# One transfer for a pair's values, and transposed keys written four columns apart

## The chip, the cores and the metric

The kernel runs on one core of a Trainium2 chip. The metric is the device time of one execution in microseconds. Three executions of the kernel before took 689.19, 692.28 and 689.82 us; their median is 689.82.

## What is computed

A block of attention, in which neighbouring queries are averaged two by two, is followed by a mixture-of-depths layer. Cut to what matters:

```
q, k, v: (8, 8, 1152, 64) float32          # batch, heads, sequence, head size
q_pool = q.reshape(B, H, S // 2, 2, D).mean(axis=3)
scores = (1 / sqrt(D)) * q_pool @ k.T      # 576 x 1152 per head
attn   = softmax(scores)
x      = (attn @ v), heads side by side    # (8, 576, 512)
score  = x @ w_gate                        # one number for a token
for each batch: the 128 tokens of highest score
    x[token] += sigmoid(score) * (relu(x[token] @ w1) @ w2)
```

A sum over all 1,152 keys does not depend on the order of the keys, as long as scores and values have the same one. The change rests on that.

## The kernel before, in words

**Pairs and half-steps.** Two heads of a batch form a pair: 8 batches of 4 pairs give 32 pairs. Each pair is worked in two halves of 288 pooled queries, so the main loop in `run` has 64 half-steps `h`. In each, TensorE multiplies keys by queries (`scores`, line 869, 36 products into nine PSUM tiles); ScalarE takes the exponential of each tile (line 876); and TensorE multiplies the half before by the values (`weighted`, line 887). Keys are taken in nine groups `c` of 128: of each group, columns `c * 128` to `c * 128 + 127` of the tile `kT` (partitions: head and feature) are the stationary operand of the scores, and the same 128 keys lie along the partitions of the tile `v_sb`, at index `c`. So column `c * 128 + m` of `kT` and row `m` of `v_sb[:, :, c, :]` must be the same key.

**Order.** The order is written out by hand: an engine does its instructions in the order in which `run` calls the functions. VectorE's share of a half-step is, in order: routing work placed at "mid" (`units`), a reduction for the gate (line 1035), two sums of exponentials by a transposing reduction (`folded`, line 913, each near 1.95 us) and a small sum (line 923), routing work placed at "sums", then in every first half `added` (line 944) and `prepare_pair` of the next pair, then the transpose of the outputs (`drained`, line 966). GpSimd adds exponentials (line 908), pools queries (line 767) and adds the two halves of the outputs (line 897).

**Preparing a pair.** `prepare_pair` is called in the first half-step of the pair before: GpSimd adds neighbouring queries into `qp`, VectorE transposes the keys `kb` into `kT` in blocks of 32 x 32 (line 770), then `qp` into `qT` (line 774). Their scores begin two half-steps later. There are 31 such pairs; the first one is prepared by other code (`load_first`, `prepare_first`), with TensorE's transposes, and its values come in by line 807 in natural order.

**Transfers.** Nearly all are issued by SP, in the order of the calls: in every second half-step the keys of the pair after the next (four transfers, line 742), its queries (four, line 745), the next pair's values (`load_values`, four, line 756), and the results of an earlier pair (four stores, line 1024). In between come the small transfers of routing: `row<-total` and its way back (lines 1094 to 1098), `row_rank<-both` and `lines<-row_rank` (1194 and 1198), `copy<-xe` and its way back (1269 and 1282). Some of these wait for VectorE, or for the transfer just before them, and SP waits with them. `kb` and `v_sb` have two buffers, `qb` has one.

**Routing.** When the four pairs of a batch are done, its tokens are ranked on VectorE (lines 1145 to 1192, result `both`), written to memory and read back as `lines`, searched (line 1229), and the chosen rows fetched. The fetched rows of most batches are transposed by VectorE into `xeT` (line 1284). Two batches at a time then pass through seven products per layer on TensorE (line 1437), with sums on GpSimd (line 1403) and VectorE (line 1450).

**Where a key goes.** In `kb` partition `i` of a block of 32 holds 36 keys in a row, key `i * 36 + n`, and the change's code reads `n` as `g * 9 + c` with `g` of 0 to 3. Block `(c, g)` is transposed as one 32 x 32 block. Before, its 32 columns are written side by side, at `c * 128 + g * 32 + i`, so row `g * 32 + i` of the values must hold key `i * 36 + g * 9 + c`. That is why the values come by four transfers, one for each `g`, each over 32 partitions.

Of the kernel before, what the change touches and what calls it, by code (L numbers as in the profile page):

```python
# [10 lines left out]
P = 128  # L11
BLK = 32
# [15 lines left out]
def _any_scores(  # L28
# [451 lines left out]
    in_pair = [(j, t) for j in range(2) for t in range(NF)] + [(0, NF)]  # L480
    upcoming = load_pair(*pairs[0])
    run(prepare_pair(upcoming))
    preparing = iter(())
    routing = iter(())
# [23 lines left out]
    for n, (b, hp) in enumerate(pairs):  # L508
        pair = upcoming
        run(preparing)  # L510
        if hp == 0:
            x = xpool.tile([P, NT, Dm], F32, name="x")
        for i, (j, t) in enumerate(in_pair):
            now = {"pair": pair, "j": j, "t": t, "x": x}
            advance(now)
            if two is not None and two["t"] == NF and two["pair"]["hp"] == NPAIR - 1:
                run(routing)
                routing = routed(two["pair"]["b"], two["x"])
            one, two = now, one
            if i == 0 and n + 1 < len(pairs):  # L520
                upcoming = load_pair(*pairs[n + 1])
                preparing = prepare_pair(upcoming)
            if n == 0 and i == 0:
                load_weights()
            if i >= 3:
                next(preparing, None)
            next(routing, None)
# [7 lines left out]
class _Plain:  # L535
# [212 lines left out]
    def load_values(self, pair):  # L748


        nc, hp = self.nc, pair["hp"]
        v_sb = pair["v"] = self.load.tile([P, 2, self.NC, self.D], F32, name="v_sb", bufs=2)
        of = self.v[pair["b"], 2 * hp : 2 * hp + 2]
        of = of.rearrange("j (i g c) d -> g i j c d", i=BLK, c=self.NC)
        for g in range(P // BLK):
            nc.sync.dma_start(
                v_sb[g * BLK : (g + 1) * BLK, :, :, :].rearrange("i j c d -> i j (c d)"),
                of[g].rearrange("i j c d -> i j (c d)"),
            )

    def prepare_pair(self, pair):

        nc = self.nc
        qp = self.load.tile([P, self.QB, BLK], F32, name="qp", bufs=1)
        kT = pair["kT"] = self.load.tile([P, self.S], F32, name="kT")
        qT = pair["qT"] = self.load.tile([P, self.Sp], F32, name="qT")
        nc.gpsimd.tensor_tensor(  # L767
            out=qp[:, :, :], in0=pair["q"][:, :, 0, :], in1=pair["q"][:, :, 1, :], op=ALU.add
        )
        nc.vector.transpose(  # L770
            kT.rearrange("p (c g i) -> p c g i", c=self.NC, i=BLK),
            pair["k"].rearrange("p (g c) d -> p c g d", c=self.NC),
        )
        nc.vector.transpose(qT[:, :], qp.rearrange("p n d -> p (n d)"))  # L774
# [971 lines left out]
```

## Time and profile before

The profiled execution took 689.66 us, of which the profile's span covers 687.9. The page gives the busy time of each engine, and then the costliest groups of instructions: for each a line of the program, the engine, what it writes and reads, how often, the busy time in all, the mean of one, and the idle time of the engine just before them with what ended it.

| what | number |
|---|---|
| span; profiled execution; median of three | 687.9; 689.66; 689.82 us |
| TensorE's granted clock over the span | 0.998 |
| ScalarE, exponentials (L876), 576 | 320.4 us, 699 ns each |
| TensorE, values (L887) and scores (L869), 4,608 each | 296.7 and 296.4 us, 403 ns each |
| VectorE, transposing reductions (L913), 128 | 250.7 us, near 1.96 us each |
| VectorE, transpose of queries (L774), 31 | 22.6 us, 730 ns each |
| values' transfers (L756), 124 of 144 KB | median 3.5 us from issue to landing |
| keys' transfers (L742), 124 of 144 KB | median 4.5 us |
| DMA moved over the span | 101.22 MB, 147 GB/s |

Instructions of TensorE overlap, so their busy times add up to more than its stretch of time, and its busy share is no measure of its efficiency. Idle time before an instruction matters only where the engine is the one that the rest waits for.

### The profile page before, as it was taken

To read this page: it belongs to the slowest core of one execution; us is meant where nothing else is said; L and a number is where in the kernel's file an instruction comes from. 1 tells how busy PE (TensorE), PEld (TensorE's weight loads), DVE (VectorE), ACT (ScalarE), POOL (GpSimd) and SP (SyncE) were. 2 spreads that over 40 slices of the span, in tenths; PEclk is the share of its full clock that TensorE was granted. 3 is DMA by queue.
4 is the path that set the end of the run, shared out by engine and by line. 5 is a ranking of instruction groups with operands and counts; after the bars stand their busy time and mean duration, and the time that the engine had idled before them with its cause. 6 is when DMAs were issued, how large, how long until landed. Compare 5 with 4: busy or idle time off the path is not lost.

```text
span 687.9 us, 23660 instructions
## 1 busy us (share of the span) xinstructions
PE 678.0 (99%) x9972; PEld 564.4 (82%) x9972; DVE 536.4 (78%) x842; ACT 457.7 (67%) x998; POOL 512.9 (75%) x503
## 2 busy tenths in 40 slices
PE   9999999999999999999999999999999999999996
PEld 6668899989997998786888899777788899867776
DVE  3867888998999796786698977695879989688930
ACT  5677777777777783847777677583877777575220
POOL 4788888798887775867996978483999888569241
PEclk9999999999999999999999999999999999999999
DMA  9888878688779767953878787783777777644311
GB/s 173 158 176 182 209 143 202 130 155 165 138 167 171 159 136 140 229 101 80 227 129 176 135 166 148 139 197 64 158 190 171 140 152 163 118 116 118 81 47 36
DMA packets 397059, 101.22 MB, mean 147 GB/s; under 512 B 377232, under 2 KB 381200, under 8 KB 395664
## 3 DMA queue, kind: packets, MB, share of 16 engines
q1 hardware_dynamic: 395408, 95.13, 67.1%
q0 software_dynamic: 1296, 4.20, 1.9%
q8 instruction: 80, 1.31, 0.8%
q10 hardware_dynamic: 240, 0.30, 0.2%
q14 instruction: 35, 0.29, 0.1%
HBM read 81.97 MB, written 17.62 MB: 145 GB/s over the span
## 4 chain that ended last, share of the span: by engine, by line
PE 83%; DVE 4%; DMA 4%; issue 4%; POOL 3%; ACT 1%; SPq 0%; POOLq 0%; DVEq 0%; ACTq 0%
PE ps L887 36%; PE ps L869 36%; PE ps L1437 8%; DVE fold L913 2%; DMA out_dram<-xe,index 1%; PE ps L1312 1%; POOL acc L908 1%; ACT p L876 1%; DMA v_sb<-in_v_dram 1%; DMA lines<-row_rank 1%; PE ps L616 1%; DMA row_rank<-both 0%; POOL prod L976 0%; POOL s L1403 0%; DVE pick L1164 0%
## 5 line engine op out<-in xcount | busy, mean ns | idle before, releaser
L876 ACT ACTIVATE p<-ps 128x576 f32<-128x576 f32 x576 | 320.4, 699 | 2.4 <-PE ps L869 2.4
L887 PE MATMUL ps<-p,v_sb 64*64 64x288 f32 x4608 | 296.7, 403 | 2.0 <-DMA v_sb<-in_v_dram 2.0
L869 PE MATMUL ps<-qT,kT 64*64 64x288 f32 x4608 | 296.4, 403 | 0.7 <-DVE token L637 0.5
L908 POOL TENSOR_TENSOR acc<-p 128x576 f32<-128x576 f32 x192 | 272.0, 1444 | 26.7 <-ACT p L876 26.1
L887 PEld LDWEIGHTS ps<-p,v_sb 64*64 64x64 f32 x4608 | 233.7, 133 | 49.9 <-ACT p L876 13.3
L869 PEld LDWEIGHTS ps<-qT,kT 64*64 64x64 f32 x4608 | 229.3, 133 | 51.4 <-ACT p L876 4.6
L913 DVE TRANSPOSE_TENSOR_REDUCE fold<-p 128x54 f32<-128x1728 f32 x64 | 126.0, 1968 | 32.8 <-ACT p L876 32.8
L913 DVE TRANSPOSE_TENSOR_REDUCE fold<-acc 128x54 f32<-128x1728 f32 x64 | 124.7, 1948 | 27.3 <-POOL acc L908 27.3
L895 ACT COPY two<-ps 128x576 f32<-128x576 f32 x64 | 40.8, 637 | 139.0 <-PE ps L887 131.6
L897 POOL TENSOR_TENSOR av<-two 128x288 f32<-128x288 f32 x64 | 51.2, 800 | 68.7 <-ACT two L895 65.4
L767 POOL TENSOR_TENSOR qp<-qb 128x576 f32<-128x576 f32 x31 | 43.7, 1409 | 14.0 <-DMA qb<-in_q_dram 12.9
L976 POOL TENSOR_TENSOR prod<-avb,w_gate 128x288 f32<-128x288 f32 x64 | 51.7, 808 | 1.5 <-DVE red L1035 1.3
L966 DVE STREAM_TRANSPOSE avb<-av 128x288 f32<-128x288 f32 x64 | 29.0, 453 | 23.2 <-POOL av L897 22.8
L770 DVE STREAM_TRANSPOSE kT<-kb 128x1152 f32<-128x1152 f32 x31 | 42.1, 1357 | 0.0
L953 ACT ACTIVATE sums<-total,tiny 32x18 f32<-32x18 f32 x124 | 38.2, 308 | 2.3 <-DVE total L944 0.3
L1013 POOL TENSOR_TENSOR x<-avb,rec 128x576 f32<-128x576 f32 x30 | 34.8, 1160 | 0.0
L1164 DVE SCALAR_TENSOR_TENSOR pick<-sc_row,gate_sc,before 128x128 f32<-128x128 f32 (+1 forms) x40 | 31.3, 782 | 1.4
L938 ACT COPY groups<-sum 32x36 f32<-32x36 f32 x124 | 27.3, 220 | 2.4 <-DVE sum L923 0.7
L1035 DVE TENSOR_REDUCE red<-prod 128x9 f32<-128x288 f32 x64 | 27.7, 433 | 0.1
L1445 ACT COPY s<-ps 128x256 f32<-128x256 f32 (+1 forms) x27 | 11.4, 447 | 20.8 <-PE ps L1437 20.8
L774 DVE STREAM_TRANSPOSE qT<-qp 128x576 f32<-128x576 f32 x31 | 22.6, 730 | 2.1 <-POOL qp L767 2.0
L923 DVE TENSOR_REDUCE sum<-fold 128x18 f32<-128x108 f32 x64 | 21.9, 342 | 2.2
(136 smaller groups left out, 481.7 us busy)
## 6 DMA issues: line engine op xcount, KB each, us to landing
kb<-in_k_dram SPq DMA_DIRECT2D x124, 144.0 KB, 4.5
qb<-in_q_dram SPq DMA_DIRECT2D x124, 144.0 KB, 3.7
v_sb<-in_v_dram SPq DMA_DIRECT2D x124, 144.0 KB, 3.5
tw<-tw SPq DMA_DIRECT2D x10, 1024.0 KB, 7.0
out_dram<-x SPq DMA_DIRECT2D x128, 72.0 KB, 3.0
lines<-row_rank SPq DMA_DIRECT2D x7, 640.0 KB, 4.6
w<-in_moe_w_dram SPq DMA_DIRECT2D x8, 512.0 KB, 6.3
tw<-tw SPq DMA_DIRECT2D x8, 512.0 KB, 5.6
```

The lines of the kernel that those rows point to most:

```text
L767: nc.gpsimd.tensor_tensor(out=qp[:, :, :], in0=pair["q"][:, :, 0, :], in1=pair["q"][:, :, 1, :], op=ALU.add)
L770: nc.vector.transpose(kT.rearrange("p (c g i) -> p c g i", c=self.NC, i=BLK), pair["k"].rearrange("p (g c) d -> p c g d", c=self.NC),)
L869: nc.tensor.matmul(sc[keys, j, 0:n], lhsT=pair["kT"][rows, c * P + keys.start : c * P + keys.stop], rhs=pair["qT"][rows, qs], start=True, ...
L876: nc.scalar.activation(p[:, c // G, c % G, :, :], sc[:, :, 0:n], AF.Exp, scale=self.scale)
L887: nc.tensor.matmul(av[j * self.D : (j + 1) * self.D, e, 0:n], lhsT=half["pair"]["v"][keys, j, c, :], rhs=half["p"][keys, c // G, c % G, j, :],
L895: nc.scalar.copy(two[:, :, :], av[:, :, 0:n])
L897: nc.gpsimd.tensor_tensor(out=half["av"][:, :], in0=two[:, 0, :], in1=two[:, 1, :], op=ALU.add)
L908: nc.gpsimd.tensor_tensor(out=acc[:, u, :], in0=units[:, 0, u, :], in1=units[:, 1, u, :], op=ALU.add)
L913: nc.vector.tensor_reduce(fold[:, a, :], of.rearrange("p u (m d) -> p (u m) d", d=BLK), AX.X, ALU.add, apply_transpose=True,)
L953: self.nc.scalar.activation(tot[rows, :], pair["total"][:, j * self.QB : (j + 1) * self.QB], AF.Identity, bias=self.tiny[0:BLK, 0:1],)
L976: self.nc.gpsimd.tensor_tensor(out=pair["prod"][:, ns, :], in0=pair["avb"][:, ns, :], in1=self.w_gate[:, hp : hp + 1, :].broadcast_to([P, ...
L1437: nc.tensor.matmul(args[0], lhsT=args[1], rhs=args[2], start=k == 0, stop=k == n - 1)
```

## The change

The values of a pair are loaded by one transfer over all 128 partitions: partition `p` takes keys `p * 9` to `p * 9 + 8` of each of the two heads, 2,304 bytes in a row from each. Row `p = 4 * i + g` then holds key `i * 36 + g * 9 + c`. To match, the transposed block `(c, g)` of the keys is written to columns `c * 128 + 4 * i + g`: its 32 columns lie four float32 apart, and the four blocks `g` of a group interleave. What is read, and the number of elements, stay the same. Nothing else is changed; the first pair keeps its own code.

```diff
@@ load_values
         v_sb = pair["v"] = self.load.tile([P, 2, self.NC, self.D], F32, name="v_sb", bufs=2)
         of = self.v[pair["b"], 2 * hp : 2 * hp + 2]
-        of = of.rearrange("j (i g c) d -> g i j c d", i=BLK, c=self.NC)
-        for g in range(P // BLK):
-            nc.sync.dma_start(
-                v_sb[g * BLK : (g + 1) * BLK, :, :, :].rearrange("i j c d -> i j (c d)"),
-                of[g].rearrange("i j c d -> i j (c d)"),
-            )
+        nc.sync.dma_start(
+            v_sb.rearrange("p j c d -> p j (c d)"), of.rearrange("j (p c) d -> p j (c d)", c=self.NC)
+        )
@@ prepare_pair
         nc.vector.transpose(
-            kT.rearrange("p (c g i) -> p c g i", c=self.NC, i=BLK),
+            kT.rearrange("p (c i g) -> p c g i", c=self.NC, i=BLK),
             pair["k"].rearrange("p (g c) d -> p c g d", c=self.NC),
         )
```

## The prediction

> **What bounds the kernel.** I read the busy shares first, then the groups, then two tables by time: what TensorE waited for, and how late VectorE's keys come.
>
> ```profile
> PE 678.0 (99%) x9972; PEld 564.4 (82%) x9972; DVE 536.4 (78%) x842; ACT 457.7 (67%) x998; POOL 512.9 (75%) x503
> ...
> L887 PE MATMUL ps<-p,v_sb 64*64 64x288 f32 x4608 | 296.7, 403 | 2.0 <-DMA v_sb<-in_v_dram 2.0
> ...
> L966 DVE STREAM_TRANSPOSE avb<-av 128x288 f32<-128x288 f32 x64 | 29.0, 453 | 23.2 <-POOL av L897 22.8
> L770 DVE STREAM_TRANSPOSE kT<-kb 128x1152 f32<-128x1152 f32 x31 | 42.1, 1357 | 0.0
> ```
>
> TensorE is busy from 1 us to about 682: anything that helps must shorten one of its few waits, anything that harms must make a new one. Of its waits, the one on v_sb (L887) belongs to the change. It falls in two places. Half-steps begin 8.73 us apart, but scores at 205.79 are followed by the next at 216.44, and those at 373.24 by 382.95: 1.92 + 0.98 = **2.9 us lost to late values, all that the transfer can win**. The first of them, in the chain of waits (start, length, what):
>
> ```profile
> 207.83 0.42 SPq L756
> 208.25 0.04 issue
> 208.30 0.43 SPq L756
> 208.72 0.04 issue
> 208.77 3.60 DMA v_sb<-in_v_dram
> 212.36 0.14 issue
> 212.50 1.64 PE ps L887 x21
> ```
>
> **The transfer.** Per pair, four issues on SP (median 427 ns and some 40 ns between) become one: 31 pairs, 93 issues fewer. Bytes and runs (256 of 2,304 bytes) stay. One issue with 256 runs: the w2 loads at L694 have as many, median 540 ns; I take 0.6. So SP gains 4 x 0.47 - 0.6 = 1.3, and 1.5 against the 2.1 us that the four take where SP is late. Landing: values of 144 KB take 3.5 us, those of 288 KB at the start 4.0, a transfer of 640 KB (L1198) 4.6. For 576 KB that gives 4.6 to 5.0; one transfer issued at 207.1 lands at 207.1 + 0.6 + 4.6 = 212.3, against 212.36 for the last quarter now. **By itself the merged transfer lands no sooner**; TensorE even loses the small start (four matmuls at 211.32) that the first two quarters let it make. The Trainium skill's "SBUF — State Buffer" (The DMA setup-cost knee) says to coalesce into the largest transfer over 128 partitions. By its fit of 2 us plus bytes over 436 GB/s, landing would be 3.35 us, some 1.2 sooner; rows of this trace with a like size say 4.6, and I use those.
>
> What is left is that SP reaches the load sooner:
>
> ```profile
> 186.20 2.45 SPq L756 DMA_DIRECT2D v_sb<-in_v_dram  x4
> 188.76 3.54 SPq L1024 DMA_DIRECT2D out_dram<-x  x4
> 192.34 0.62 SPq L725 DMA_DIRECT2D tw<-tw  x1
> 193.06 0.40 SPq L1094 DMA_DIRECT2D row<-total  x1
> 195.48 0.34 SPq L1095 DMA_DIRECT2D sc_row<-row  x1
> ```
>
> SP runs back to back here. The load of values at 186.20 is over 1.5 us sooner, so `row<-total` is (its total was ready by 184.5), so is its landing, for which L1095 waits 1.9, so are keys, queries and the values at 207.08: stall 1.92 - 1.5 = 0.4. The same at 350.72 for the stall at 373. The other end: the 16 DMA engines are 79% busy in this stretch, and issues stretch where they are full (one L756 took 2,277 ns); then SP's saving turns into waiting, and the gain is 0. Ends 0 and 2.9; the middle, **1.5 us gained**. Queued behind the load on SP are the stores (L1024) and, in some steps, routing's small transfers; they come sooner by as much.
>
> **The transpose.** Reads stay as they are; writes now step 16 bytes. A contiguous one of 288 columns takes 453 ns, of 1,152 takes 1,357: 904/864 = 1.046 ns a column and 152 ns fixed. The trace has one transpose that writes with this same step (L1284, `p c (j b) -> p c b j`, b = 4), and a copy from PSUM that only writes with a step (L1126, 18 columns):
>
> ```profile
> L1284 DVE STREAM_TRANSPOSE xeT<-pick 128x512 f32<-128x512 f32 x6 | 7.2, 1194 | 0.0
> L1126 DVE COPY sc_row<-ps 128x288 f32<-128x288 f32 x1 | 0.7, 694 | 0.1
> ```
>
> L1284: (1194 - 152)/512 = 2.03 ns a column, twice the contiguous. It reads with a step of 16 bytes too, so if the read alone were to blame, the new transpose would cost nothing more. L1126 reads in order and still takes 694 where contiguous copies of 192 and 384 columns (357 and 552 ns) put 288 at 455. So the write pays. New duration 152 + 1152 x 2.03 = 2.49 us, **+1.13 us each**; ends 0 and 1.13. The skill's SBUF page (Door 1: The DMA port swizzle) weighs in on both sides: it says that a 16-byte line needs two hits to run at full rate, and also that a stride of 4 fp32 is free. By the second the change costs nothing; L1284 answers for the first.
>
> 31 x 1.13 = 35 us more of VectorE, 78% to 83% of the span. That is no bound by itself. What counts is what waits for it: kT and then qT (L774, next on the queue), for which scores (L869) wait two half-steps on. I compared, for all 31 pairs, the end of qT with the first matmul of its scores. Most have 1.58 us or more to spare, up to 16. Seven are the tight ones, or follow a full stretch: those with qT ending at 251.10 (0.66 spare), 273.28 (0.17), 346.09 (0.96), 416.57 (1.70), 439.35 (0.61), 512.73 (0.83), 605.20 (0.69). The tightest, in the timeline:
>
> ```profile
> 270.95 0.39 DVE L944 TENSOR_REDUCE total<-groups 32x36 f32<-32x144 f32 x1
> 271.27 1.36 DVE L770 STREAM_TRANSPOSE kT<-kb 128x1152 f32<-128x1152 f32 x1
> 272.56 0.72 DVE L774 STREAM_TRANSPOSE qT<-qp 128x576 f32<-128x576 f32 x1
> ...
> 273.45 0.91 PE L869 MATMUL ps<-qT,kT 64*64 64x288 f32 x12
> ```
>
> Before each of 273, 346, 439 and 512 VectorE waits over 2 us on ACT's or GpSimd's work (or runs on results of TensorE's products just made), so it arrives on time and only its own 1.13 counts: 0.96 + 0.17 + 0.52 + 0.30 = **1.95 us of new TensorE waits**. At 605: 0.44, but the end is set by VectorE from 607.74, where it waits 2.54 for GpSimd, and TensorE later waits 0.16 and 0.42 for VectorE; covered, 0.
>
> At 251 and 416 lateness carried from earlier pairs matters, since VectorE is nearly full in routing. From 120 to 249 it works 117 of 129 us. Transposes at 138, 156 and so on each add 1.13 with no wait between them to absorb it. What absorbs it is the wait for `lines<-row_rank` (3.3 us at 158, 5.0 at 230, 4.0 at 397, 2.7 at 562). That transfer is set by SP, which reaches it 4 us after VectorE's `both` is done (151.0 to 155.07, 223.2 to 227.99). So lateness ends there: at 230, 3.1 late (1.95 left after qT's wait for GpSimd at 210, plus 1.13), and 5.0 absorbs it. At 251 then: 1.13 - 0.66 = 0.47, and at 257 xeT (L1284) feeds GpSimd's sums, whose first ends 0.4 before TensorE's product, 0.26 more: 0.73. If SP comes 1.5 sooner, lines do, VectorE starts them at 233.8, ahead of its old time, and nothing is lost. Half: **0.35**. At 416: 1.13 < 1.70, none.
>
> **The sum.** 1.95 + 0.35 - 1.5 = +0.8. The profiled execution took 689.66 (span 687.9 and 1.75 around it), 0.16 under the median of 689.82. 689.66 + 0.8 = 690.5, against the median 690.6; I say **690.7**, a little up because the small early start of the weighted sums goes too.
>
> **Rivals.**
> - *Lateness carries* (slower). If the wait for lines passes VectorE's delay on, or operations with two inputs stretch when they meet GpSimd (L1229 took 0.89 us at 161.40 and 3.00 at 167.41; L1164 0.35 to 1.5), the delays of 138 to 249 add up: 2.66 late after 156, 3.8 after 175 against 2.2 spare (stall 1.6), then 3.3 against 2.24 (1.1), at 251 2.4 + 0.26, at 416 0.3, plus 1.95 and 0.44 at 605: 8.0, and with no gain 697.7. It decides once VectorE is more than about 4 us late at `both`. Half of it gives 693.7. For: VectorE's load of 91% there. Against: SP's 4 us of spare.
> - *The write step is free* (faster). Then the gain alone: 689.66 - 2.9 = 686.8 at best. For: L1284 has a stepped read too. Against: L1126.
> - *SP gains nothing* (full DMA engines): 1.95 + 0.73 + 0.44 = 3.1, 692.8. For: 79% DMA share. Against: four issues of 0.42 back to back at 207.
> - *Neither part does what it says*: 689.7; nothing speaks for it, since the shapes are plain in the diff.
>
> **Numbers.** The measurement tells 0.5% apart, 3.45 us: faster is below 686.4, slower above 693.3. Forecast (gain and loss nearly cancel) 0.47, its own range 688.5 to 692.8; SP gains nothing 0.15; lateness carries 0.28; free write 0.09; nothing 0.01. Within the bound lie 0.43 of the forecast (0.01 faster, 0.03 slower), 0.12 of the second (0.03 slower), 0.02 of the third (0.26 slower), 0.03 of the fourth (0.06 faster) and all of the last: faster 0.07, same 0.61, slower 0.32. The range runs from 687.5 (free write, most of the gain) to 696.0 (three quarters of the carried lateness).
>
> **What would show it.** L770's mean at 2.4 to 2.5 us; L756 31 times, 0.5 to 0.7 us each, landing in 4.5 to 5; TensorE waiting for VectorE's qT or kT before L869 at four or five places, 0.2 to 1.0 us each, first near 273; the waits for v_sb under 1.5 us in sum. I am wrong if L770 stays below 1.6 us, if L869's waits pass 4 us, or if values come later than now.

## The result and the profile after

Over 22 executions of each kernel the median went from 692.54 to **688.53 us: ratio 0.995, 95% interval 0.9929 to 0.9972**. The forecast was no change that can be measured, at 690.7. The gain of 4.0 us is small, but its interval leaves 1 out. Single executions overlap: 688.84 to 698.72 us before, 686.68 to 693.42 after. The profiled executions differ by less: 689.66 before, 688.53 after. Why these two gaps are not the same is half of what the experiments found.

The page of the kernel after, with the rows that answer to those of before (line numbers are three lower):

```profile
PE 676.1 (98%) x9972; PEld 456.0 (66%) x9972; DVE 564.4 (82%) x842; ACT 458.4 (67%) x998; POOL 516.0 (75%) x503
...
L866 PE MATMUL ps<-qT,kT 64*64 64x288 f32 x4608 | 293.0, 403 | 2.3 <-DVE qT L771 1.6
L884 PE MATMUL ps<-p,v_sb 64*64 64x288 f32 x4608 | 291.6, 403 | 0.6 <-DMA v_sb<-in_v_dram 0.6
...
L767 DVE STREAM_TRANSPOSE kT<-kb 128x1152 f32<-128x1152 f32 x31 | 73.2, 2363 | 0.0
```

VectorE's transpose of keys costs about what was forecast: 2.36 us instead of 1.36, where 2.49 was expected. TensorE's wait for values fell from 2.0 to 0.6 us, and a wait of 1.6 us for transposed queries is new; it is a single one. In the timeline of TensorE (start, length, instructions) the stall at 211 is gone; two lines of before, then after:

```profile
205.79 4.62 PE L869 MATMUL ps<-qT,kT 64*64 64x288 f32 x72
...
216.44 0.42 PE L869 MATMUL ps<-qT,kT 64*64 64x288 f32 x2
```

```profile
205.91 4.55 PE L866 MATMUL ps<-qT,kT 64*64 64x288 f32 x72
210.27 4.55 PE L884 MATMUL ps<-p,v_sb 64*64 64x288 f32 x72
214.64 4.55 PE L866 MATMUL ps<-qT,kT 64*64 64x288 f32 x72
```

Scores follow scores after 8.73 us, where before it was 10.65 (205.79 to 216.44). From there the kernel after is 1.80 us ahead, and 1.84 still at 505. Then it gives this back: the scores due at 511.7 begin at 513.47, after a wait of 1.58. At the last half-step the two are level to 0.1 us. The last microsecond of the 1.13 is in the tail; a second profile of before has the same short tail, so it is not put down to the change. **In this one pair of executions the main loop gained nothing; over many executions the kernel gained 4.0 us.**

The other thing to see is when SP reaches the values. From SP's timeline, four of the eleven loads up to 210 us, first before, then after:

```profile
94.27 2.09 SPq L756 DMA_DIRECT2D v_sb<-in_v_dram  x4
...
134.66 3.03 SPq L756 DMA_DIRECT2D v_sb<-in_v_dram  x4
...
168.25 2.11 SPq L756 DMA_DIRECT2D v_sb<-in_v_dram  x4
...
207.08 2.11 SPq L756 DMA_DIRECT2D v_sb<-in_v_dram  x4
```

```profile
93.54 0.93 SPq L754 DMA_DIRECT2D v_sb<-in_v_dram  x1
...
131.30 1.37 SPq L754 DMA_DIRECT2D v_sb<-in_v_dram  x1
...
163.94 0.67 SPq L754 DMA_DIRECT2D v_sb<-in_v_dram  x1
...
201.40 1.01 SPq L754 DMA_DIRECT2D v_sb<-in_v_dram  x1
```

SP is 0.7 us earlier at the 5th load, 3.4 at the 7th, 4.3 at the 9th and 5.7 at the 11th. **Part of each pair's saving is kept for the next**: some 0.8 us a pair from the 5th to the 11th. Landing itself became slower, 3.5 to 5.2 us median, for a transfer four times as large.

### The profile page after: what moved, and what is told of

It is laid out like the page before. It is cut to its first block, busy times and chain, and to the rows that moved or that the text cites. A ratio compares the mean times of both kernels' runs of the same rounds, so it can differ in the third digit from the quotient of the medians.

```text
span 686.8 us, 23542 instructions
## 1 busy us (share of the span) xinstructions
PE 676.1 (98%) x9972; PEld 456.0 (66%) x9972; DVE 564.4 (82%) x842; ACT 458.4 (67%) x998; POOL 516.0 (75%) x503
## 4 chain that ended last, share of the span: by engine, by line
PE 89%; DMA 5%; POOL 2%; issue 2%; DVE 1%; ACT 1%; ACTq 0%; POOLq 0%; DVEq 0%
PE ps L884 38%; PE ps L866 38%; PE ps L1434 11%; DMA out_dram<-xe,index 2%; PE ps L1309 1%; POOL acc L905 1%; DMA v_sb<-in_v_dram 1%; DMA xe<-out_dram,index 1%; DMA p<-in_q_dram 1%; POOL qp L764 0%; POOL xe L1494 0%; DMA out_dram<-lines,index_part 0%; ACT p L873 0%; DVE kT L767 0%; POOL prod L973 0%
## 5 line engine op out<-in xcount | busy, mean ns | idle before, releaser
L905 POOL TENSOR_TENSOR acc<-p 128x576 f32<-128x576 f32 x192 | 276.1, 1465 | 27.6 <-ACT p L873 27.3
L866 PE MATMUL ps<-qT,kT 64*64 64x288 f32 x4608 | 293.0, 403 | 2.3 <-DVE qT L771 1.6
L884 PE MATMUL ps<-p,v_sb 64*64 64x288 f32 x4608 | 291.6, 403 | 0.6 <-DMA v_sb<-in_v_dram 0.6
L866 PEld LDWEIGHTS ps<-qT,kT 64*64 64x64 f32 x4608 | 177.6, 133 | 105.3 <-ACT p L873 17.2
L884 PEld LDWEIGHTS ps<-p,v_sb 64*64 64x64 f32 x4608 | 176.9, 133 | 103.3 <-ACT p L873 14.7
L767 DVE STREAM_TRANSPOSE kT<-kb 128x1152 f32<-128x1152 f32 x31 | 73.2, 2363 | 0.0
L1161 DVE SCALAR_TENSOR_TENSOR pick<-sc_row,gate_sc,before 128x128 f32<-128x128 f32 (+1 forms) x40 | 33.0, 824 | 1.4
```

Of the source, the lines that this page charges most:

```text
L767: nc.vector.transpose(kT.rearrange("p (c i g) -> p c g i", c=self.NC, i=BLK), pair["k"].rearrange("p (g c) d -> p c g d", c=self.NC),)
L866: nc.tensor.matmul(sc[keys, j, 0:n], lhsT=pair["kT"][rows, c * P + keys.start : c * P + keys.stop], rhs=pair["qT"][rows, qs], start=True, ...
L884: nc.tensor.matmul(av[j * self.D : (j + 1) * self.D, e, 0:n], lhsT=half["pair"]["v"][keys, j, c, :], rhs=half["p"][keys, c // G, c % G, j, :],
L905: nc.gpsimd.tensor_tensor(out=acc[:, u, :], in0=units[:, 0, u, :], in1=units[:, 1, u, :], op=ALU.add)
```

## The experiments

Each run's ratio is to runs of the kernel before on the same chip. Three theories stood at the start: SP's issue time (four issues against one), the transfer (partitions, length of the runs, landing), and the transpose (a cost, or a layout that helps elsewhere).

### Each part alone

The stepped transpose with four transfers of 32 partitions each; the values lie as in the kernel after. It was run again later, beside other kernels.

```diff
-        nc.sync.dma_start(v_sb.rearrange("p j c d -> p j (c d)"), of.rearrange("j (p c) d -> p j (c d)", c=self.NC))
+        of = of.rearrange("j (p c) d -> p j (c d)", c=self.NC)
+        for g in range(P // BLK):
+            rows = slice(g * BLK, (g + 1) * BLK)
+            nc.sync.dma_start(v_sb[rows, :, :, :].rearrange("p j c d -> p j (c d)"), of[rows])
```

> The stepped transpose without the merged load: values in the new order, but by four transfers over 32 partitions. Theory (SP's queue: the gain is SP's time, the transpose costs a few waits of TensorE for qT): no gain is left, so 0.2 to 0.5% slower than before (ratio 1.002 to 1.005), L767 at 2.36 us, and stalls for v_sb of 2 to 4 us as before. Rival (the stepped transpose costs nothing or even helps by shifting VectorE): ratio 0.998 to 1.001. Rival (lateness carries): ratio above 1.01.

> The stepped transpose with four transfers over 32 partitions once more, beside the two others on one chip. Both theories: as in its first run, ratio to before 0.999 to 1.004, with waits for values near the 23rd half-step.

Measured: 1.0008 (0.9978 to 1.0038) and 1.0001 (0.9968 to 1.0033). The waits for values are back (2.9 us, five times, in the second). The first had been expected to be 0.2 to 0.5% slower. So the transpose gains nothing, and costs too little to be resolved.

The one transfer with the old transpose. Values then meet other keys, so this kernel computes another function with the same work.

```diff
-            kT.rearrange("p (c i g) -> p c g i", c=self.NC, i=BLK),
+            kT.rearrange("p (c g i) -> p c g i", c=self.NC, i=BLK),
```

> The merged load alone: the changed kernel with the old transpose, whose columns lie side by side. Values then meet other keys than their own, so the output is another function; the amount of work is that of the kernel. Theory (SP's time is the gain, the stepped transpose a loss of about 1.5 us): 0.6 to 0.9% faster than before (ratio 0.991 to 0.994), no waits of TensorE for qT of over 0.5 us. Rival (the stepped transpose costs nothing): the same as the changed kernel, 0.995. Rival (the stepped transpose carries the gain): ratio 0.998 or more.

> The changed kernel once more, beside the others on one chip. Theory: ratio 0.993 to 0.997, values leave SP at least 3 us before they are needed for every pair (before: 1.0 and 1.6 us for the 11th and 19th), and waits for qT between 1 and 3 us in sum, in places that differ from the first profile's. Rival (the gain was a chance of the chip): ratio above 0.998.

Measured on one chip: the transfer alone 687.74 us, 0.9925 (0.9897 to 0.9952); the kernel after 688.05, 0.993 (0.9904 to 0.9955). The transfer is the whole gain. The transpose costs 0.3 us at these medians; as the seven executions of each overlap (686.55 to 689.11 and 687.27 to 688.61), that is less than the runs can tell.

### Is it the transfer's form, or the number of issues?

Two kernels keep the layout and the transpose of the kernel after, and issue four transfers again: over all 128 partitions (by head, five and four groups), or over 64 partitions with runs of 2,304 bytes as in the one transfer.

```diff
+        of = of.rearrange("j (p c) d -> p j c d", c=self.NC)
+        for j in range(2):
+            for cs in (slice(0, 5), slice(5, self.NC)):
+                nc.sync.dma_start(v_sb[:, j, cs, :].rearrange("p c d -> p (c d)"), of[:, j, cs, :].rearrange("p c d -> p (c d)"))
```

```diff
+        of = of.rearrange("j (p c) d -> j p (c d)", c=self.NC)
+        for j in range(2):
+            for rows in (slice(0, P // 2), slice(P // 2, P)):
+                nc.sync.dma_start(v_sb[rows, j, :, :].rearrange("p c d -> p (c d)"), of[j, rows])
```

> The changed kernel, with its values loaded by four transfers again, but each over all 128 partitions (split by head and into 5 and 4 of the nine groups, so runs of 1,280 and 1,024 bytes; twice as many runs). Theory (SP's time counts, about 2.5 us a pair in the loaded stretch for four issues against 0.9 for one): SP spends as long on values as before, falls behind, and the gain goes, ratio to before 0.998 to 1.003. Rival (what counts is that a transfer over 32 partitions loads the DMA side worse than one over 128): the gain stays, 0.993 to 0.996, with four issues.

> The changed kernel with its values by four transfers over 64 partitions, one head each, so 256 runs of 2,304 bytes as in the merged one, but four issues. Theory (number of issues): the gain goes, ratio to before 0.998 to 1.003, spare of the values for the 11th pair 3 us or less. Rival (shorter runs cost the run with four transfers over 128 partitions its gain): ratio 0.992 to 0.996.

Measured: 0.9991 (0.9961 to 1.0021) and 1.0041 (1.0015 to 1.0068), the second above the 1.003 expected at most. With four issues the gain is gone, whatever the partitions or runs. The two profiles lie at opposite ends of their twelve executions. That of the first took 686.66 us, the lowest (median 691.85), and shows no wait for values: even with four issues, values are late in some executions and not in others. That of the second took 698.82, the highest (median 694.42); SP reaches the 11th load at 209.97, where the four profiles of before have 207.1 to 209.7. Its own row (count, least/median/largest ns) beside that of the kernel after:

```profile
L757 SPq DMA_DIRECT2D v_sb<-in_v_dram x124: 465/596/3216, 26.2 to 617.4; - x124
```

```profile
L754 SPq DMA_DIRECT2D v_sb<-in_v_dram x31: 382/931/2728, 26.8 to 606.1; - x31
```

Mean times matter more than medians here: from the start of a pair's first issue to the end of its last SP spends 3.14 us in the one, 0.96 in the other, and 2.69 in the kernel before.

### Giving SP's time back in doses

The kernel after, with three, five or nine transfers of one number each behind the values' transfer.

```diff
+        for _ in range(3):   # 5, 9
+            i = self.n_small = getattr(self, "n_small", -1) + 1
+            nc.sync.dma_start(self.scratch[i % 3 : i % 3 + 1, i // 3 : i // 3 + 1], self.w_gate_in[i : i + 1].unsqueeze(0))
```

> The changed kernel, with three transfers of one number each issued on SP behind each load of values, so that SP issues as often as before while the merged load stays. Theory (the gain is SP's time, gathered over several pairs): values and keys leave SP as late as before from the routing of the first batch on, waits for v_sb of 1 us or more come back, and most of the gain goes: ratio to before 0.998 to 1.002. Rival (the gain is one landing instead of four, or 128 partitions at once): the gain stays, ratio 0.994 to 0.996.

> The changed kernel with five transfers of one number behind each load: 1.5 us of SP a pair, about what the merged load saved. Theory (SP's time, of which the changed kernel has some 0.8 us a pair to spare in the loaded stretch): part or all of the gain goes, ratio to before 0.995 to 1.002. Rival (SP's time is free up to here): 0.991 to 0.995.

> The changed kernel with nine transfers of one number behind each load of values (0.3 us of SP each, 2.7 a pair), so that SP spends more on them and the merged load together than the kernel before did on four. Three such transfers cost nothing. Theory (SP's time): the values' spare for the 7th and 11th pair falls from 7.6 and 7.9 us to 2 or less, ratio to before 0.999 to 1.004. Rival (the DMA side): the gain stays, 0.991 to 0.996, and SP merely waits less for full DMA queues.

Three: 687.0, **0.9916** (0.9886 to 0.9947); the gain stays, against what was expected, though SP gives back half of the time saved. Five: 694.03, 1.0047 (1.0016 to 1.0078). Nine: 740.37, 1.0677 (1.0638 to 1.0716). The last two are slower than either reading had it. They gave more of SP's time than they were meant to, as the waits of SP (what waited, for what, us in all, times, longest) show for five:

```profile
SPq L1025 <- DMA v_sb<-in_v_dram: 27.7, 28, 1.9
```

The store behind the five small transfers waited for the landing of the values, 0.9 us a pair. With nine, the small ones themselves waited (13.2 us from 20 to 215), and one pair's nine took 3.8 to 6.2 us. In both, the values still come by one transfer over 128 partitions and the gain is gone, so the single landing is not the gain. Taken as SP's time per pair, waits within it included, the runs fall in order (each time from one profile, each ratio from all executions):

| kernel | SP's time on values and small transfers, per pair | ratio |
|---|---|---|
| after; again | 0.96; 1.03 us | 0.995; 0.993 |
| three small | 1.91 | 0.9916 |
| transpose only, four of 32 partitions; again | 2.52; 2.69 | 1.0008; 1.0001 |
| before; four of 128 partitions | 2.69; 2.72 | 1; 0.9991 |
| four of 64 partitions | 3.14 | 1.0041 |
| five small, with the stores' wait | 3.4 | 1.0047 |
| nine small | 5.6 | 1.068 |

The step lies between 1.9 and 2.5 us. Four transfers a pair, when three are cheap, keep the gain, so it is SP's time and not their number. Why 1.9 costs nothing is in SP's waits from 20 to 215 us in the kernel after:

```profile
SPq L754 <- PE ps L866: 4.9, 8, 0.9
SPq L745 <- POOL acc L905: 4.3, 8, 0.9
```

SP is so far ahead that it waits for buffers: 9.2 us in some twelve pairs, 0.8 a pair to spare (before: 2.9 us for the same two).

### Is it only that values come late?

The kernel before, and the one after, with the values' transfers called ahead of the next keys and queries.

```diff
-                if n + 2 < len(pairs):
-                    loaded = self.load_pair(*pairs[n + 2])
                 if n + 1 < len(pairs):
                     self.load_values(upcoming)
+                if n + 2 < len(pairs):
+                    loaded = self.load_pair(*pairs[n + 2])
```

> The kernel before, with the load of a pair's values called ahead of the load of keys and queries, so that it leaves SP some 9 us sooner; four transfers and the old transpose. Theory (late values cost the time): no wait of TensorE for v_sb, 0.4 to 0.8% faster than before (ratio 0.992 to 0.996), about as fast as the changed kernel or faster. Rival (SP's total time matters, not the place of the values): keys and queries are late instead, ratio 0.998 to 1.003. Rival (the gain came from anything else): ratio 1.000.

> The changed kernel, with the load of values called ahead of keys and queries. Theory: the changed kernel has at most 0.6 us of waits for values left, so this gives under 0.1% against it (ratio to before 0.993 to 0.996). Rival (values were still late in most executions of the changed kernel): ratio under 0.993.

Measured: 1.0065 (1.0038 to 1.0093) and 0.9984 (0.9954 to 1.0014). The first had been expected to gain. Its profile is of the longest of its twelve executions (699.93 us, median 695.99). TensorE's waits in it, and GpSimd's for the queries:

```profile
PE ps L869 <- DVE qT L774: 6.3, 6, 2.5
PE ps L1437 <- POOL s L1403: 2.8, 2, 1.7
...
POOL qp L767 <- DMA qb<-in_q_dram: 39.0, 14, 7.0
```

In the kernel before the last of these rows is:

```profile
POOL qp L767 <- DMA qb<-in_q_dram: 12.9, 7, 3.9
```

No wait for values is left, and 9.1 us of others came. Putting values first moves SP's lateness to the queries, which is worse. The stall on values was where an overfull SP showed.

### The new wait for queries

The kernel after, with the transpose of keys called ahead of the sums of exponentials (`folded`) in first half-steps; queries follow where they were.

```diff
+            if s == 0 and loaded:
+                self.prepare_keys(loaded)
             self.folded(half)
```

> The changed kernel, with VectorE's transpose of the keys called ahead of the sums of exponentials of the same half-step, so that only qT is left behind them. Theory (the stepped transpose costs where scores wait for qT at the end of that row): those waits shrink from some 2 us to under 0.5, ratio to before 0.991 to 0.994. Rival (the sums are then late and ScalarE or GpSimd wait, or keys have not landed): ratio 0.995 or more.

Measured: 686.41 us, 0.991 (0.9879 to 0.9942), the lowest median of all; the kernel after had 688.05 on that chip, and as the two intervals overlap, the step beyond it is not resolved. TensorE's waits have no queries among them:

```profile
PE ps L888 <- DMA v_sb<-in_v_dram: 1.5, 1, 1.5
```

### What one profile of before did not show

The kernel before, profiled three more times.

> The kernel before once more, to see what differs between its executions. Theory (its slower executions have more or longer waits for values): ratio 1.000, and another execution's profile shows waits for v_sb in other places or of other size than the 1.92 and 0.98 us of the first. Rival (its spread comes from the tail's transfers): the same two waits, and a different time from 605 us on.

> The kernel before, unchanged, in a third profiled execution. Open is why its median over many executions (692.5) lies 2.9 us above its first profile (689.66). Theory: the price of late values differs between executions, because a stall of 2 us or more is in some of them followed by TensorE's granted clock of 0.5 to 0.8 for some 4 us. Then an execution near 692 shows stalls on v_sb with 2 us more loss in all than the first profile's 2.9 (half-steps longer than 8.73 us), and a granted clock under 0.85 behind at least one of them. Rival: the difference is spread over the span or lies in the tail, and the half-steps with late values lose 2.9 us or less.

> The same kernel once more, with the same two readings: time above 689.7 found again as longer half-steps where values are late (theory), or not there (rival). If this execution is near 689.7, the theory wants stalls of 3 us or less in all and no fall of the clock.

These executions took 691.26, 695.57 and 697.96 us; the first of the three was also timed against itself, 0.9986 (0.9958 to 1.0015). The extra time sits where values are late. TensorE's timeline in the fourth, around the 27th pair, where the first profile had no stall at all:

```profile
542.16 4.76 PE L869 MATMUL ps<-qT,kT 64*64 64x288 f32 x72
549.46 0.70 PE L887 MATMUL ps<-p,v_sb 64*64 64x288 f32 x4 [2.54 <-DMA v_sb<-in_v_dram]
551.05 6.03 PE L887 MATMUL ps<-p,v_sb 64*64 64x288 f32 x66 [0.89 <-DMA v_sb<-in_v_dram]
556.68 0.42 PE L869 MATMUL ps<-qT,kT 64*64 64x288 f32 x2
```

and its stretches (busy time of each engine, then TensorE's granted clock, DMA share, GB/s):

```profile
542.00:546.00 4.00, 4.00 (x72) 2.62 (x64) 3.65 (x4) 3.21 (x7) 0.00 (x0) 1.00 0.82 129
546.00:550.00 4.00, 1.46 (x20) 0.43 (x12) 0.54 (x2) 3.77 (x10) 1.73 (x2) 1.00 0.99 216
550.00:554.00 4.00, 3.12 (x30) 2.16 (x32) 3.93 (x12) 0.00 (x0) 4.00 (x4) 0.66 0.79 126
```

This half-step takes 14.52 us, 5.79 more than 8.73: 2.54 and 0.89 of waiting, and 66 products that take 6.03 us instead of 4.34, since the clock fell to 0.66 behind the gap. SP reached these values at 545.47; in the first profile it did at 537.29, in the third at 546.40. Of these 8 to 9 us TensorE's own delay up to there is 2.4 and 4.2; SP came 5 to 6 us later than that. **How late SP is differs that much between executions of one kernel.**

| profile of before | time | half-steps with over 0.5 us lost at late values | sum | over the first: time; losses |
|---|---|---|---|---|
| first | 689.66 us | 1.92, 0.98 | 2.90 | |
| second | 691.26 | 4.11 | 4.11 | 1.6; 1.2 |
| third | 695.57 | 4.42, 2.68 | 7.10 | 5.9; 4.2 |
| fourth | 697.96 | 1.19, 2.31, 0.68, 5.79 | 9.97 | 8.3; 7.1 |

The second is nearest to the median of 692.54; the third and fourth are long executions. Most of what a longer execution of before has more is late values, and part of that is the clock. In the two profiles of the kernel after, the half-step that ends near 381 is 0.8 and 0.2 us over 8.73, and no other place waits for values.

## Why the prediction was wrong, step by step

- **"What is left is that SP reaches the load sooner"** held: the gain goes with SP's issue time, not with the landing, for which "no sooner" was right (5.2 us from the start of the issue; before, the four quarters for the stall at 211 took 5.3 together). The sum added 0.6 us of issue to rows of 4.6 us that already count from the issue; the landing proved slower than those rows by as much. SP's time per pair fell by 1.7 us where the sum had 1.3 to 1.5.
- **The gain of 1.5 us is the step that failed, twice.** On one chip the transfer alone gained 5.4 us (693.11 to 687.74), and the whole change gave -4.0 us where the sum had +0.8. The sum let SP's saving count once, for one pair ahead of the stall. But SP's queue was full from pair to pair, and in the profile after the lead grew to 5.7 us by the 11th load; the stall there went from 1.92 to 0, not to 0.4. And the ceiling "2.9 us, all that the transfer can win" came from one execution. In three others the same mechanism lost 4.1, 7.1 and 10.0 us, so what could be won was larger than the profile at hand showed.
- **The base.** 689.66 and the median of 689.82 over three lay low: the median over 22 is 692.54, and the four taken beside the experiments lie at 691.94 to 693.11. A kernel with a stall of varying size needs more than three executions for a base.
- **The transpose.** 2.49 us forecast from L1284, 2.36 measured: with the reads unchanged, the write step makes 1.36 into 2.36. The sentence of the Trainium skill's "SBUF — State Buffer" (Door 1: The DMA port swizzle) that calls a step of four fp32 free does not hold for this operation. The rival of the free write is out. That 688.53 lies in the range given, near its lower end of 687.5 that stood for this rival, is luck.
- **New waits of 1.95 us for queries.** Near in sum by luck (one wait of 1.58 in the profile), and wrong in place. Over many executions next to nothing of this loss is seen: 0.3 us at the medians of the kernels with and without the stepped write. The ends of qT at 273, 439 and 605 were compared with the scores next in time, which belong to the second half of the pair before; their own scores had 8.9 to 9.4 us to spare. So 0.96 + 0.52 of the 1.95 were never at risk. Of the other two, the scores after 346 came 0.26 late (0.17 forecast; 0.93 in the second profile of after), and at 512 the wait was 1.58 instead of 0.30. There VectorE was late already, by a wait for GpSimd, before the longer transpose came on top. GpSimd itself had waited 1.33 and 1.08 us for indirect transfers of routing, and with the one transfer and the old transpose the scores here follow the end of the queries by 0.15 us, where before it was 0.83. VectorE's timeline after:

```profile
507.70 1.98 DVE L910 TRANSPOSE_TENSOR_REDUCE fold<-acc 128x54 f32<-128x1728 f32 x1 [4.67 <-POOL acc L905]
...
510.47 2.27 DVE L767 STREAM_TRANSPOSE kT<-kb 128x1152 f32<-128x1152 f32 x1
512.60 0.72 DVE L771 STREAM_TRANSPOSE qT<-qp 128x576 f32<-128x576 f32 x1
```

- **0.35 us at 251.** The end of that estimate with no loss came true: queries end 3.62 us before their scores where it was 0.66.
- **Rivals.** Lateness of VectorE did not carry: up to 500 us the profile lists no wait for queries. "SP gains nothing" is out: the one transfer alone gains, and with four issues the gain is gone. Whether the lost start on the first two quarters costs anything was not tried by itself.

Not settled: the transpose's exact cost, and what sets SP's lateness apart from one execution of a kernel with four issues to the next.

## What to carry to other kernels

If the issuing queue is full, count its issue time per repetition and let the saving add up until something, a buffer or a landing, makes the queue wait; where it then waits is the end of the gain. Do not take the size of a stall from one execution: ask how much spare the neighbouring places have, because the next execution may lose there. And compare an operand's end with the scores of its own pair, not with the next ones in time.

## What the runs showed of the hardware

- After a gap of TensorE the granted clock fell in some cases and not in others. Waits of 1.49 + 0.40 us (second profile of before) were followed by 0.64 over 4 us, and 2.10 us (four of 64 partitions, at 521) by 0.59 over 4 us and 72 products in 6.29 us instead of 4.54; a wait of 2.54 us in the kernel with values first (at 220) was followed by 1.00. The Trainium skill's "TensorE: Matmul & The Clock Gate" (Why this matters for your kernels) warns of gaps over about 3 us; here shorter ones sufficed.
- Transfers of one number issue in about 0.25 us each, but from five behind a large one SP began to wait for landings. It is seen in two kernels and not explained.
- TensorE's weight loads show 456 us of busy time after and 564 before, with equal counts and 133 ns each; the matmuls stay at 403 ns. It goes with the partitions that a transfer of values covers, not with the number of transfers or the transpose: 543 to 564 us in every profile with transfers over 32 partitions, 495 with 64, and 454 to 472 with 128, the four issues over 128 among them (461). It is not explained, and no time was seen to hang on it.
